# Moving a fold from GpSimd to VectorE in spread pieces, and halving the block sums, in a mixer kernel

## The chip, the cores and the metric

The kernel runs on one core of a Trainium2 chip; every trace and result lists that core alone. The metric is the device time of one execution in microseconds (us), lowest is best. Every kernel is timed beside runs of the kernel before on the same chip. Engines: PE is TensorE's matrix multiply, PEld its weight load, DVE is VectorE, ACT is ScalarE, POOL is GpSimd, SP is the engine that only issues DMAs here.

## The reference, cut to what matters

```python
X = np.fft.fft(x, axis=1); X = np.fft.fft(X, axis=2); x = X.real   # x: 8 x 3008 x 256
xt = x.transpose(0, 2, 1)
h = np.maximum(xt @ w_tok1, 0.0) @ w_tok2        # token mixing, 3008 -> 256 -> 3008
u = x + h.transpose(0, 2, 1)
h2 = np.maximum(u @ w_ch1, 0.0) @ w_ch2          # channel mixing, 256 -> 1536 -> 256
return (u + h2).astype(np.float32)
```

The kernel works batch by batch. While TensorE does the channel mixing of batch b (six chunks of 512 tokens, the last of 448, each in four "places" s = 0 to 3, so 24 places a batch), the Fourier front end of batch b+1 is woven in, and before that the input x of batch b+2 is *folded*: x[t] plus or minus x[-t], which halves the work of the transform.

## The kernel before

Three parts matter. The first is the fold, 12 pieces a batch, on whatever engine is handed in. Every operand is fp16 in SBUF:

```python
def fold(b, engs):
    ...
    for s, (t0, t1) in enumerate(((13, 17), (9, 13), (5, 9), (1, 5))):
        tt = engs[s].tensor_tensor
        ...
        tt(out=xp[:, t, 1:D], in0=xp[:, t, 1:D], in1=xm[0:KR, rv, D - 1:0:-1], op=add)   # L423
        yield
        ...
        tt(out=eo[:, t, 1:129], in0=xp[:, t, 1:129], in1=xp[:, t, 255:127:-1], op=add)   # L429
        yield
        tt(out=eo[:, t, 129:256], in0=xp[:, t, 1:128], in1=xp[:, t, 255:128:-1], op=sub) # L431
        yield
```

The second is the block sums on VectorE. The second channel product is done with seven block products instead of eight, which needs four sums of blocks of the hidden layer c1 in each of 42 of the 48 chunks (the other six, `plain` in the code, take the eight products). All operands are in SBUF again:

```python
def hidden_sums(c1, sb, k, which):
    ...
    sums = ((sb[:, 0, k], a21, a22, AT.add),                 # sb<-c
            (sb[:, 1, k], sb[:, 0, k], a11, AT.subtract),    # sb<-sb,c
            (a21, a11, a21, AT.subtract),                    # c<-c
            (sb[:, 2, k], a12, sb[:, 1, k], AT.subtract))    # sb<-c,sb
    for i in which:
        o, x, y, op = sums[i]
        nc.vector.tensor_tensor(out=o, in0=x, in1=y, op=op)  # L609
```

The third is the second product. TensorE's results are added up by VectorE out of PSUM (`residual(v, ...)`), and GpSimd adds the transposed u, `rt`, from SBUF to SBUF (`residual(g, ...)`, both L618). VectorE first copies some edge columns of `rt` (`edges`, L613). PSUM for this product has only two buffers, so TensorE waits when VectorE's residual add is late (13 waits, 23.5 us in all, in the trace of this kernel).

```python
elif s == 2:
    product(pa[:, 0], lambda k: c1[:, k], 1, lambda k: wst[:, 2, k])
    keep(2)
    residual(v, osb[:, 2:4, upper], pb[:, 0], m[:, 2])
else:
    product(pa[:, 0], ...); product(pb[:, 0], ...)
    residual(v, osb[:, 2:4, lower], pa[:, 0], rt[:, 2:4, lower])
    residual(v, osb[:, 0:2, upper], pb[:, 0], m[:, 1])
    residual(g, osb[:, :, upper], osb[:, :, upper], rt[:, :, turned_])
```

The main loop before: fold 1 runs on GpSimd ahead of the loop, folds 2 to 7 two pieces a place from place 10 (batch 0: 15), and the four block sums of a chunk run whole in places 0 and 1 of the next chunk.

## Time and profile before

643.45 us, median of 3 runs (643.16 to 644.06).

| | before |
|---|---|
| PE busy | 595.9 us, 93% of the span (642.3 us, the profiled run) |
| DVE, ACT, POOL busy | 482.5, 442.7, 296.9 us |
| batches 0 to 7 | 74.5, 77.4, 77.8, 76.9, 77.7, 74.9, 71.2, 67.2 us |
| PE gaps in them | 3.0, 4.5, 5.7, 5.7, 4.5, 3.8, 0, 0.1 us |

A batch is measured from its first up-projection matmul (L592) to that of the next; batch 7 ends with PE's last work. A gap is the time from the end of PE's last matmul to the start of its next; the ends are modelled.

From the page of the kernel before: the engines' busy time, and the busy tenths in 40 equal slices. PEclk is the granted clock in tenths.

```profile
PE 595.9 (93%) x6322; PEld 425.1 (66%) x6322; DVE 482.5 (75%) x820; ACT 442.7 (69%) x996; POOL 296.9 (46%) x261
...
PE   2899989998899988999888998999989999999997
POOL 8459269337932378104991159601692211111121
PEclk9999989999899999999999999899999999999999
```

PE is the bound. After start-up it falls to 8 in nine slices, and in eight of these POOL is at 6 or more; but in three of the seven slices in which POOL reaches 9, PE stays at 9. In three places the clock falls too, to 0.5 for 3.41 us each.

Windows cut at the batches (kernel before; start:end, length, then busy us and instruction count of each engine, granted clock, DMA share, GB/s): batches 1, 2, 6 and 7.

```profile
core 0: us, PE busy (x) PEld busy (x) DVE busy (x) ACT busy (x) POOL busy (x), PEclk, DMA share, GB/s
114.40:191.80 77.40, 72.95 (x757) 51.21 (x756) 57.14 (x93) 51.91 (x119) 41.04 (x34) 0.98 0.57 102
191.80:269.60 77.80, 72.09 (x806) 51.81 (x805) 63.85 (x96) 52.92 (x122) 39.20 (x32) 1.00 0.39 83
499.00:570.30 71.30, 71.30 (x806) 51.68 (x805) 52.89 (x96) 52.76 (x122) 12.28 (x12) 1.00 0.33 68
570.30:637.50 67.20, 67.14 (x673) 47.69 (x671) 44.19 (x76) 42.99 (x88) 13.60 (x11) 1.00 0.35 76
```

Batches 2 and 6 do the same work on PE (806 matmuls), yet batch 2 takes 6.5 us more. DVE runs the same 96 instructions in both, and is busy 63.85 us in one and 52.89 in the other. The difference between the batches is the fold on POOL, with the load of x that batch 2 issues behind it; batch 5 folds and issues no load, and still has 3.8 us of gaps.

The list of PE's waits (kernel before; total us, times, longest):

```profile
PE px L633 <- DVE osb L618: 23.5, 13, 2.9
PE pt L265 <- ACT tp L249: 11.7, 1, 11.7
```

The second line is start-up. The first is nearly the whole of what the batches lose.

Groups of instructions by form (kernel before; out<-in, count, busy us, mean ns, then idle time before them):

```profile
L609 DVE TENSOR_TENSOR sb<-sb,c 128x1536 f16<-128x1536 f16 x42 | 64.7, 1540 | 1.4
L609 DVE TENSOR_TENSOR c<-c 128x1536 f16<-128x1536 f16 x42 | 50.8, 1211 | 0.0
L613 DVE COPY rt<-rt 128x4 f16<-128x4 f16 x72 | 28.8, 400 | 0.8
...
L423 POOL TENSOR_TENSOR xp<-xp,xm 94x1020 f16<-94x1020 f16 x28 | 66.3, 2367 | 7.2 <-PE filler L283 7.2
```

The means hide two populations. A sum that no POOL op overlaps takes 0.95 us; one that POOL ops cover for 95% or more takes 1.5 to 2.1 us on average, by kind of sum. VectorE's adds out of PSUM take the same alone and so covered: 0.42 us for 128x256 (`osb`), 0.69 for 128x512 (`ut`).

One such case in the timeline of the kernel before (start us, length us; lines picked from it):

```profile
164.73 1.86 POOL L431 TENSOR_TENSOR eo<-xp 94x508 f16<-94x508 f16 x1
165.78 2.92 DVE L613 COPY rt<-rt 128x4 f16<-128x4 f16 x2
166.18 0.83 PE L633 MATMUL py<-wst,sb 128*128 128x128 f16 x12
166.56 2.11 POOL L423 TENSOR_TENSOR xp<-xp,xm 94x1020 f16<-94x1020 f16 x1
168.61 0.41 DVE L618 TENSOR_TENSOR osb<-px,m 128x256 f32<-128x256 f32 x1
169.07 0.44 PE L633 MATMUL px<-wst,sb 128*128 128x128 f16 x5 [2.06 <-DVE osb L618]
```

Two copies of four columns, 0.17 us each when undisturbed, last until the fold piece is done. The residual add behind them is 2 us late, and PE stands for 2.06 us.

### The profile page before, as it was taken

Reading aid. Unit: us, or ns where it says so; the run is one execution under the profiler, and the core shown is the slowest. Engines: PE = TensorE matmul, PEld = TensorE weight load, DVE = VectorE, ACT = ScalarE, POOL = GpSimd, SP = SyncE. Lnnn points to the kernel's source line nnn. Section 1 sums busy time; section 2 is a strip of 40 time slices with the busy share of each in tenths; the row PEclk is TensorE's granted clock in tenths of the full one; section 3 lists DMA queues with packets and bytes.
Section 4 is the critical chain, followed back from the end, with each engine's and each line's share of the span. In section 5 each row is a group of like instructions: output and inputs, shape, how many; then the busy total and the mean of one; then the engine's idle time right before and its main releaser. Section 6 shows DMA issues by size and latency. Waiting matters only on the chain.

```text
span 642.3 us, 15533 instructions
## 1 busy us (share of the span) xinstructions
PE 595.9 (93%) x6322; PEld 425.1 (66%) x6322; DVE 482.5 (75%) x820; ACT 442.7 (69%) x996; POOL 296.9 (46%) x261
## 2 busy tenths in 40 slices
PE   2899989998899988999888998999989999999997
PEld 1766667665677656766666665776667767766675
DVE  8667678569777798757979589765997766776764
ACT  8766966676568765777665866668667777766672
POOL 8459269337932378104991159601692211111121
PEclk9999989999899999999999999899999999999999
DMA  9993921952353325352264322832403342322423
GB/s 141 210 181 87 174 50 35 166 83 59 59 126 82 85 51 103 90 99 50 51 119 112 70 57 44 172 72 49 94 17 73 66 92 59 72 62 58 96 55 97
DMA packets 86599, 56.51 MB, mean 88 GB/s; under 512 B 54864, under 2 KB 83472, under 8 KB 85776
## 3 DMA queue, kind: packets, MB, share of 16 engines
q1 hardware_dynamic: 78048, 37.84, 28.5%
q0 software_dynamic: 8256, 17.49, 15.7%
q8 instruction: 49, 0.80, 0.5%
q10 hardware_dynamic: 224, 0.20, 0.1%
q14 instruction: 22, 0.18, 0.1%
HBM read 34.98 MB, written 24.64 MB: 93 GB/s over the span
## 4 chain that ended last, share of the span: by engine, by line
PE 74%; DVE 13%; issue 5%; ACT 5%; POOL 2%; DVEq 0%; POOLq 0%
PE pc L592 31%; PE px L633 18%; PE py L633 6%; PE pu L552 6%; PE po L690 4%; DVE sb L609 3%; PE pt L488 3%; DVE c L609 2%; DVE osb L618 2%; PE pz L445 2%; ACT c L595 1%; DVE ut L560 1%; DVE rt L613 1%; DVE ut L544 1%; POOL xp L423 1%
## 5 line engine op out<-in xcount | busy, mean ns | idle before, releaser
L595 ACT ACTIVATE c<-pc 128x512 f16<-128x512 f32 (+1 forms) x572 | 296.4, 595 | 41.7 <-PE pc L592 22.1
L618 POOL TENSOR_TENSOR osb<-osb,rt 128x256 f32<-128x256 f32 x84 | 89.6, 1067 | 312.7 <-DVE osb L618 303.2
L592 PE MATMUL pc<-ut,wc1p 128*128 128x512 f16 x576 | 140.3, 379 | 0.0
L592 PE MATMUL pc<-ut,wc1m 128*128 128x512 f16 (+1 forms) x576 | 137.9, 376 | 0.0
L633 PEld LDWEIGHTS <-c 128*128 128x128 f16 x2016 | 121.2, 98 | 23.8 <-DVE c L609 5.7
L633 PEld LDWEIGHTS <-sb 128*128 128x128 f16 x1512 | 91.1, 98 | 34.5 <-issue 22.9
L638 ACT ACTIVATE m<-px 128x256 f32<-128x256 f32 x126 | 48.5, 385 | 94.5 <-PE px L633 71.0
L560 DVE TENSOR_TENSOR ut<-pu,yt 128x512 f16<-128x512 f32 (+1 forms) x96 | 64.3, 672 | 31.5 <-PE pu L552 31.3
L592 PEld LDWEIGHTS <-wc1m 128*128 128x128 f16 x576 | 53.7, 99 | 47.9 <-issue 3.0
L592 PEld LDWEIGHTS <-wc1p 128*128 128x128 f16 x576 | 52.2, 98 | 49.0 <-issue 2.2
L633 PE MATMUL px<-wst,c 128*128 128x128 f16 x1008 | 70.5, 220 | 2.5 <-DVE c L609 2.1
L423 POOL TENSOR_TENSOR xp<-xp,xm 94x1020 f16<-94x1020 f16 x28 | 66.3, 2367 | 7.2 <-PE filler L283 7.2
L609 DVE TENSOR_TENSOR sb<-sb,c 128x1536 f16<-128x1536 f16 x42 | 64.7, 1540 | 1.4
L633 PE MATMUL px<-wc,c 128*128 128x128 f16 x1008 | 63.1, 219 | 0.0
L609 DVE TENSOR_TENSOR sb<-c 128x1536 f16<-128x1536 f16 x42 | 54.4, 1295 | 7.5 <-ACT c L595 7.5
L633 PE MATMUL px<-wst,sb 128*128 128x128 f16 x504 | 36.0, 222 | 23.5 <-DVE osb L618 23.5
L609 DVE TENSOR_TENSOR sb<-c,sb 128x1536 f16<-128x1536 f16 x42 | 53.6, 1277 | 0.0
L290 ACT ACTIVATE z<-pz 128x480 f16<-128x480 f32 (+1 forms) x60 | 40.1, 674 | 18.9 <-PE pz L445 9.8
L618 DVE TENSOR_TENSOR osb<-py,m 128x256 f32<-128x256 f32 x84 | 35.4, 422 | 23.5 <-ACT m L638 13.0
L609 DVE TENSOR_TENSOR c<-c 128x1536 f16<-128x1536 f16 x42 | 50.8, 1211 | 0.0
L552 PE MATMUL pu<-w2p,uu 128*128 128x512 f16 (+1 forms) x168 | 50.3, 379 | 0.2 <-ACT uu L510 0.2
L431 POOL TENSOR_TENSOR eo<-xp 94x508 f16<-94x508 f16 (+1 forms) x28 | 44.2, 1578 | 0.0
(168 smaller groups left out, 762.9 us busy)
## 6 DMA issues: line engine op xcount, KB each, us to landing
out_dram<-osb SPq DMA_DIRECT2D x83, 256.0 KB, 3.5
xp<-in_x_dram POOLq DMA_DIRECT2D x16, 272.0 KB
out_dram<-osb SPq DMA_DIRECT2D x11, 192.0 KB, 3.2
xp<-in_x_dram POOLq DMA_DIRECT2D x16, 127.5 KB
rt<-ut SPq DMA_TRANSPOSE x96, 3.1
w2s<-in_moe_w_tok_dram POOLq DMA_DIRECT2D x1, 1504.0 KB
w1p<-in_moe_w_tok_dram POOLq DMA_DIRECT2D x2, 384.0 KB
wc<-in_moe_w_ch_dram POOLq DMA_DIRECT2D x1, 768.0 KB
```

Source lines behind the costliest of these rows:

```text
L290: nc.scalar.activation(out=out_, in_=in_, func=AFT.Copy)
L423: tt(out=xp[:, t, 1:D], in0=xp[:, t, 1:D], in1=xm[0:KR, rv, D - 1:0:-1], op=add)
L431: tt(out=eo[:, t, 129:256], in0=xp[:, t, 1:128], in1=xp[:, t, 255:128:-1], op=sub)
L552: nc.tensor.matmul(pu[:, 0:n], lhsT=uu[:, th, int(minus), h, :], rhs=w2_cols(b, c)[:, th], start=(th == 0), stop=(th == 1))
L560: nc.vector.tensor_tensor(out=ut[:, h, 0:n].rearrange("p (a b) -> p a b", b=64), in0=pu[:, 0:n].rearrange("p (b a) -> p a b", b=64), in1=y ...
L592: nc.tensor.matmul(pc[:, 0:n], lhsT=wc[:, h, ct * P:(ct + 1) * P], rhs=ut[:, h, 0:n], start=(h == 0), stop=(h == 1))
L595: nc.scalar.activation(out=c1[:, ct, 0:n], in_=pc[:, 0:n], func=AFT.Relu)
L609: nc.vector.tensor_tensor(out=o, in0=x, in1=y, op=op)
L618: eng.tensor_tensor(out=o, in0=x, in1=y, op=AT.add)
L633: nc.tensor.matmul(o[:, t], lhsT=a(k)[:, f:f + P], rhs=w(k), start=(first and t == 0 and k == 0), stop=(k == HC - 1), skip_group_check=True)
L638: nc.scalar.activation(out=m[:, i], in_=pa[:, 0], func=AFT.Copy)
L690: nc.tensor.matmul(po[0:n, o:o + D], lhsT=c1[:, ct, ks * P:ks * P + n], rhs=wc2[:, ct, :], start=(ct == 0), stop=(ct == NCT - 1))
```

## The change

Its intent: take the fold off GpSimd, where it disturbs VectorE, and give it to VectorE in pieces so small and so spread that VectorE can take them; and split the block sums so that half of them run while the chunk's own relus still come, rather than all in the first half of the next chunk. The core of the diff:

```diff
-    if BB > 1:
-        take(fold(1, [nc.gpsimd] * 4), 12)
-    if BB > 2:
-        x_tiles[2] = load_x(2)
+    early = fold(1, [nc.vector] * 4)
...
-        folds = fold(b + 2, [nc.gpsimd] * 4) if b + 2 < BB else None
+        folds = fold(b + 2, [nc.vector] * 4) if b + 2 < BB else None
...
-                sums = prev is not None and not plain(*prev[0:2])
-                if s == 0 and sums:
-                    hidden_sums(prev[2], pbox["sb"], slice(0, HC), (0, 1))
+                if s < 2 and prev is not None and not plain(*prev[0:2]):
+                    block_sums(prev[2], pbox["sb"], slice(3, HC), (2 * s, 2 * s + 1))
...
-                if s == 1 and sums:
-                    hidden_sums(prev[2], pbox["sb"], slice(0, HC), (2, 3))
                 if prev is not None:
                     mm2(*prev, s, pbox)
+                if s >= 2 and not plain(b, c):
+                    block_sums(c1, box["sb"], slice(0, 3), (2 * s - 4, 2 * s - 3))
...
-                if b == 0 and sub == 5:
+                if b == 0 and sub == 4:
                     weight_sums()
...
+                if b == 0 and 3 <= sub < 9:
+                    take(early, 2)
+                    if sub == 8:
+                        x_tiles[2] = load_x(2)
                 if folds is not None and sub >= fold_at[b > 0]:
-                    take(folds, 2)
-                    if sub == fold_at[b > 0] + 5 and b + 3 < BB:
+                    take(folds, 1 + (b == 0))
+                    if sub == fold_at[b > 0] + (5 if b == 0 else 11) and b + 3 < BB:
                         x_tiles[b + 3] = load_x(b + 3)
```

(`block_sums` is `hidden_sums` renamed.) So the change has three parts: the *engine* of the fold, its *spread* (one piece a place over twelve places instead of two over six, from batch 1 on), and the *halves*. Some small moves come with them: fold 1 goes from ahead of the loop into places 3 to 8 of batch 0, the loads of x and the weight sums change places.

More of the change, by code (lines that the diff above doesn't have):

```diff
@@ L597, in mm1, with block_sums @@
                 ts(c1[:, ct, 0:n], pc[:, 0:n], 0.0, AT.max)
-    def hidden_sums(c1, sb, k, which):
+    def block_sums(c1, sb, k, which):
         hi = slice(HC + k.start, HC + k.stop)
```

## The prediction

The sum is 610 us as the ceiling (643.45 us less about 33) and 6 to 7 us given back, 616.

> **What bounds it now.** TensorE. On the page PE is busy 595.9 us of 642.3 (93%) and holds 74% of the chain of waits. By windows cut at each batch's first up-projection matmul (L592), the batches take 74.5, 77.4, 77.8, 76.9, 77.7, 74.9, 71.2 and 67.2 us. Batches 6 and 7 run no fold, and PE has no gap there. In batches 0 to 5 its gaps sum to 3.0, 4.5, 5.7, 5.7, 4.5 and 3.8 us, 27 us in all, nearly all in the second half of a batch, where GpSimd folds. The list of waits puts 23.5 us of PE's down to VectorE's residual add (`px <- osb`, L618). After three gaps the granted clock is 0.6-0.8 for about 4 us (near 90, 171, 404 us), some 5 us more.
>
> **Why VectorE is late.** A block sum takes 0.95 us with GpSimd idle; covered by a GpSimd op 1.5-2.1 us, longest 2.9. A 4-column edge copy goes from 0.17 to 1.2 us. Ops with an operand in PSUM (0.42, 0.69 us) don't change. [...] At 165.8 us two edge copies take 2.9 us beside a fold, the residual add follows, PE waits 2.06 us.
>
> **What the change moves.**
> - Folds of batches 1 to 7 leave GpSimd: about 164 of its 297 us. The residual adds (about 12 us a batch) and loads of x stay.
> - VectorE gets them. Its fold of batch 0 shows the price: 0.68, 0.43, 0.41 us a piece (2.4, 1.6, 1.6 on GpSimd), 6.8 us a batch, 47 us in all.
> - Each block sum becomes two. The weight sums (128x768, 0.56 us undisturbed) give the price: 2 x 0.56 against 0.95, at most 27 us over 168 sums, about half as back-to-back ops overlap by 0.08 us.
> - VectorE loses the fold's stretch: 63.8 us busy in batch 2, 52.9 in batch 6, so about 10 us a batch.
> VectorE's total stays near 480-510 us. TensorE's work is unchanged.
>
> **Critical path.** Against about 71.1 us (batch 6; batch 5 less its gap), batches 1 to 5 lose 6.3, 6.7, 5.8, 6.6 and 3.8 us, 29 us; batch 0 loses 3 to 4. Ceiling about 33 us, so 610. I give back about 1 us a batch, since VectorE nears 90% in chunks 2 to 5 and GpSimd's residual adds still stretch some sums, and 1 to 2 us in batch 0, where the early fold, the weight sums and the new halves fall into 16 us of a VectorE already full.
>
> **Predicted: 616 us, range 608 to 627 (8 in 10).** Faster by over 2%: 0.93; within 2%: 0.06; slower: 0.01.
>
> **Right if** batches 1 to 5 take 71 to 73 us; PE's waits on `osb` fall from 23.5 to under 6 us; GpSimd is busy 130-140 us; a half sum takes about 0.56 us, a few stretched beside L618 on GpSimd; no clock drop after 100 us; batches 6 and 7 stay within 1 us. What is left lies at 45 to 65 us and in chunks 3 to 5.
>
> **Wrong if** VectorE is full in chunks 2 to 5, so that sums or `ut` come late (then 625-635); if GpSimd's residual adds stretch the many smaller ops more than the larger; if fold 1 ends late and batch 1's front or batch 2's load waits; or if an unbroken TensorE draws a lower clock, which batches 6 and 7 (139 us near 1.0) don't show.

## The result, and the profile after

617.39 us, median of 4 runs (616.26 to 618.29), against 643.75 us (643.16 to 645.24, 4 runs). The ratio is 0.9586, 95% interval 0.9561 to 0.9612: 4.1% faster. Ratios here are the mean time of one kernel's runs over that of the other's runs of the same rounds, so not quite the ratio of the medians quoted.

From the page of the kernel after, the same lines as before:

```profile
PE 589.1 (96%) x6322; PEld 422.5 (69%) x6322; DVE 492.8 (80%) x1086; ACT 442.0 (72%) x996; POOL 139.3 (23%) x163
...
PE   2899999999999999999999999999999999999996
POOL 8500413111142121302114221311121212101121
PEclk9999999999999999999999999999999999999999
```

POOL lost 157.6 us of work, DVE gained 10.3 us in all, and no slice of PE or of its clock falls below 9 between start-up and the last slice. That the time falls by 26 us while PE's busy time falls by only 7 is no contradiction: most of the gain is PE's idle time (its gaps in batches 0 to 5 fall from 27.1 to 5.5 us). Of the 7 us of busy time the clock is about 5, by an estimate: the trace of the kernel before has three stretches of 3.41 us in the batches in which the granted clock is 0.5, that of the kernel after has none.

Windows of batches 1, 2, 6 and 7 (kernel after):

```profile
110.30:181.60 71.30, 70.97 (x758) 50.60 (x757) 57.63 (x127) 51.75 (x119) 13.65 (x15) 1.00 0.42 80
181.60:254.40 72.80, 71.74 (x805) 51.79 (x804) 62.94 (x134) 52.88 (x122) 17.26 (x19) 1.00 0.44 89
470.10:542.00 71.90, 71.51 (x805) 51.75 (x804) 57.45 (x120) 52.88 (x122) 12.97 (x12) 1.00 0.33 67
542.00:609.30 67.30, 67.11 (x672) 47.65 (x671) 47.42 (x96) 43.01 (x88) 12.54 (x11) 1.00 0.39 76
```

The eight batches take 71.9, 71.2, 72.9, 71.6, 72.9, 71.2, 71.9 and 67.3 us. DVE does the whole fold in batch 2 (134 instructions instead of 96) and is busy *less* than before, 62.94 against 63.85 us. PE's waits (kernel after):

```profile
PE px L633 <- DVE osb L618: 2.6, 8, 0.8
PE pz L445 <- DVE ut L560: 1.6, 3, 0.7
```

From the groups by form (kernel after):

```profile
L609 DVE TENSOR_TENSOR sb<-c,sb 128x768 f16<-128x768 f16 x84 | 84.4, 1004 | 0.0
L609 DVE TENSOR_TENSOR c<-c 128x768 f16<-128x768 f16 x84 | 49.5, 590 | 0.0
L609 DVE TENSOR_TENSOR sb<-sb,c 128x768 f16<-128x768 f16 x84 | 46.9, 558 | 2.9
L609 DVE TENSOR_TENSOR sb<-c 128x768 f16<-128x768 f16 x84 | 45.9, 547 | 2.4 <-ACT c L595 2.4
L613 DVE COPY rt<-rt 128x4 f16<-128x4 f16 x72 | 13.3, 184 | 0.8
```

The edge copies are free of the stretch (184 ns against 400). The half sums are at 0.55 to 0.59 us, but for one kind, `sb<-c,sb`, whose mean is 1.00 us. The timeline of the kernel after, at the start of batch 2, shows what holds it (lines picked from it):

```profile
182.01 0.41 DVE L618 TENSOR_TENSOR osb<-py,m 128x256 f32<-128x256 f32 x1
182.34 0.56 DVE L609 TENSOR_TENSOR c<-c 128x768 f16<-128x768 f16 x1
182.83 2.05 DVE L609 TENSOR_TENSOR sb<-c,sb 128x768 f16<-128x768 f16 x1
183.27 1.17 POOL L618 TENSOR_TENSOR osb<-osb,rt 128x512 f32<-128x512 f32 x1
184.79 0.68 DVE L560 TENSOR_TENSOR ut<-pu,yt 128x512 f16<-128x512 f32 x1
185.53 0.37 PE L445 MATMUL pz<-t1n,eo 94*128 94x96 f16 x5 [0.72 <-DVE ut L560]
```

GpSimd's own residual add is released by VectorE's residual add, so it starts just when the half sums behind that add run. The add of `ut` comes late, and PE waits 0.72 us for it. Chunk 0 of batches 2 and 4 takes 13.29 us in place of 12.04; g1 below takes this cause away, and chunk 0 is back at 12.04.

### The profile page after: what moved, and what is told of

Read it like the earlier page. It is cut to its first block, busy times and chain, and to the rows that moved or that the text cites. A ratio compares the mean times of both kernels' runs of the same rounds, so it can differ in the third digit from the quotient of the medians.

```text
span 614.2 us, 15694 instructions
## 1 busy us (share of the span) xinstructions
PE 589.1 (96%) x6322; PEld 422.5 (69%) x6322; DVE 492.8 (80%) x1086; ACT 442.0 (72%) x996; POOL 139.3 (23%) x163
## 4 chain that ended last, share of the span: by engine, by line
PE 80%; DVE 8%; ACT 6%; issue 3%; POOL 1%; DMA 1%; DVEq 0%; POOLq 0%
PE pc L592 33%; PE px L633 20%; PE py L633 7%; PE pu L552 6%; PE po L690 4%; PE pt L488 3%; ACT c L595 3%; DVE sb L609 2%; DVE osb L618 2%; PE pz L445 1%; PE pw L472 1%; PE pw L473 1%; DVE ut L560 1%; PE py L519 1%; DVE yt L526 1%
## 5 line engine op out<-in xcount | busy, mean ns | idle before, releaser
L618 POOL TENSOR_TENSOR osb<-osb,rt 128x256 f32<-128x256 f32 x84 | 92.2, 1097 | 438.5 <-DVE osb L618 411.4
L592 PE MATMUL pc<-ut,wc1m 128*128 128x512 f16 (+1 forms) x576 | 134.9, 370 | 0.0
L609 DVE TENSOR_TENSOR sb<-c,sb 128x768 f16<-128x768 f16 x84 | 84.4, 1004 | 0.0
L618 DVE TENSOR_TENSOR osb<-py,m 128x256 f32<-128x256 f32 x84 | 35.4, 422 | 29.4 <-ACT m L638 23.2
L609 DVE TENSOR_TENSOR c<-c 128x768 f16<-128x768 f16 x84 | 49.5, 590 | 0.0
L609 DVE TENSOR_TENSOR sb<-sb,c 128x768 f16<-128x768 f16 x84 | 46.9, 558 | 2.9
L609 DVE TENSOR_TENSOR sb<-c 128x768 f16<-128x768 f16 x84 | 45.9, 547 | 2.4 <-ACT c L595 2.4
L475 DVE SCALAR_TENSOR_TENSOR w<-alt,pw 128x131 f16<-128x131 f16 x96 | 33.0, 350 | 14.4 <-ACT w L290 14.3
L526 DVE TENSOR_TENSOR yt<-py,qs 128x512 f16<-128x512 f32 x48 | 30.8, 683 | 8.8 <-ACT qs L522 8.8
```

Of the source, the lines that this page charges most:

```text
L475: nc.vector.scalar_tensor_tensor(out=w[:, g, 0:131], in0=alt[:], scalar=pw[:, 131:132], in1=pw[:, 0:131], op0=AT.mult, op1=AT.add)
L526: nc.vector.tensor_tensor(out=yt[:, h, CW * c:CW * c + CW], in0=py[:], in1=qs[:], op=op)
L592: nc.tensor.matmul(pc[:, 0:n], lhsT=wc[:, h, ct * P:(ct + 1) * P], rhs=ut[:, h, 0:n], start=(h == 0), stop=(h == 1))
L618: eng.tensor_tensor(out=o, in0=x, in1=y, op=AT.add)
```

## The experiments

Theory A: while GpSimd reads SBUF, VectorE's ops with two SBUF inputs and its edge copies are stretched (in before the sums go from 0.95 to 1.5-2.1 us beside its ops, the copies from 0.17 to 1.2); the residual adds then come late and PE waits. That it is the read of SBUF is a supposition at this point, which e5 and e6 test. Rivals: B, the gain comes from the halves and the even spread, whatever engine folds; C, GpSimd's queue was too long, so its residual adds and stores came late.

### The engine, the spread and the halves one by one

The three parts can each be on or off, which makes eight kernels. Six were built beside before and after. All but e3 were made from the kernel after and so keep its small moves (fold 1 inside the loop, the loads, the weight sums); a comparison of e7 or e8 with before has these in it, one among e1, e2, e4, e7, e8 and after does not, but for the loads of x, which go with the spread.

e1_engine, one word undone in two places:

```diff
-    early = fold(1, [nc.vector] * 4)
+    early = fold(1, [nc.gpsimd] * 4)
-        folds = fold(b + 2, [nc.vector] * 4) if b + 2 < BB else None
+        folds = fold(b + 2, [nc.gpsimd] * 4) if b + 2 < BB else None
```

> The changed kernel with one word undone: all folds of batches 1 to 7 go back to GpSimd; the halves, the spread places and the new load places stay. Theory A (GpSimd's folds stretch VectorE's two-input ops and edge copies): most of the gain goes, 636 to 648 us; block halves beside a fold well over 0.56 us; PE gaps of 3 us or more in each of batches 1 to 5. Rival B (the halves and the even spread made the gain, whatever engine folds): 615 to 622 us.

e2_fold_only, the block sums whole again:

```diff
-                    block_sums(prev[2], pbox["sb"], slice(3, HC), (2 * s, 2 * s + 1))
+                    block_sums(prev[2], pbox["sb"], slice(0, HC), (2 * s, 2 * s + 1))
-                if s >= 2 and not plain(b, c):
-                    block_sums(c1, box["sb"], slice(0, 3), (2 * s - 4, 2 * s - 3))
```

> The changed kernel with the block sums whole again, in their old places; folds on VectorE, spread. Theory A: keeps nearly all of the gain, 614 to 622 us. Rival B: loses half or more of it, 628 us or more. If the halves cost VectorE more than they return, this run is at or below the changed kernel's 617.

e3_halves_only is the kernel before with only the two `block_sums` hunks of the change and the place of the weight sums.

> The kernel before with only the block sums halved (and the weight sums one place earlier, as the change has them); folds stay on GpSimd, two pieces a place. Theory A: within 1% of before, 637 to 648 us. Rival B: 630 us or less.

e4_burst, the spread undone:

```diff
-                    take(folds, 1 + (b == 0))
-                    if sub == fold_at[b > 0] + (5 if b == 0 else 11) and b + 3 < BB:
+                    take(folds, 2)
+                    if sub == fold_at[b > 0] + 5 and b + 3 < BB:
```

> The changed kernel with the folds of VectorE not spread: two pieces a place for six places, as before, load of x six places earlier. If the spread matters (VectorE is near full in chunks 2 to 4 and a pair of pieces delays the residual adds): 619 to 624 us, with new PE gaps in chunk 3 or 4. If it doesn't: within 1.5 us of the changed kernel.

e7_spread_only is e2 with both folds on `nc.gpsimd`; e8_engine_only is e2 with the edit of e4.

> Folds on GpSimd, but in the changed kernel's spread places (one piece a place over twelve); block sums whole as before. With e1 (0.9855 of before, with halves) it tells the part of the spread. Theory A (each piece beside VectorE costs a stretch, and two in one place cost PE a wait that one doesn't): 632 to 640 us, near e1. If the halves made e1's gain: 642 to 648.

> Folds on VectorE in the old bursts of two pieces a place, block sums whole. With e4 (halves, 0.975 of before) it tells whether halves hurt in a burst. Theory A: the engine alone gives about half of the gain, 622 to 632 us, with PE gaps left in chunks 3 and 4; the halves cost VectorE about 1.3 us a batch there, so this is some us under e4.

Measured (each ratio is to the kernel before on the same chip, whose median was 643.75 us beside after, 645.54 beside e1 to e4 and 644.02 beside e5 to e8; 95% interval in brackets; batches 1 to 5, and the sum of PE's gaps in each of them, from the traces):

| kernel | fold on | pieces | sums | median us | ratio | batches 1-5, us | PE gaps in each, us |
|---|---|---|---|---|---|---|---|
| before | GpSimd | burst | whole | 643.75 | 1 | 74.9-77.8 | 3.8-5.7 |
| e3 | GpSimd | burst | halves | 665.05 | 1.0305 (1.0279-1.0331) | 79.7-82.2 | 7.1-7.4 |
| e7 | GpSimd | spread | whole | 633.77 | 0.9843 (0.9826-0.9859) | 74.1-75.4 | 3.0-3.4 |
| e1 | GpSimd | spread | halves | 635.96 | 0.9855 (0.9827-0.9884) | 74.0-75.9 | 2.7-3.6 |
| e8 | VectorE | burst | whole | 626.32 | 0.9733 (0.9708-0.9759) | 72.5-73.3 (one 79.0) | 1.3-1.5 (one 5.2) |
| e4 | VectorE | burst | halves | 628.93 | 0.9750 (0.9706-0.9794) | 73.6-75.1 | 2.4-2.9 |
| e2 | VectorE | spread | whole | 618.41 | 0.9585 (0.9568-0.9602) | 71.8-72.4 | 0.7-0.8 |
| after | VectorE | spread | halves | 617.39 | 0.9586 (0.9561-0.9612) | 71.2-72.9 | 0.3-1.1 |

What follows:

- The engine gives 2.6 to 2.7% with whole sums (e8 against before; e2 against e7) and the spread 1.5 to 1.6% (e7 against before; e2 against e8). With whole sums they add up; neither alone is the change. (The spread alone is under 2%, but its interval excludes 1.) Theory A as stated put the gain down to the engine alone, and e1 came out at the edge of what it allowed (635.96 us, expected 636 to 648; gaps of 3 us or more expected, 2.7 to 2.8 found in batches 1, 3 and 5): a part of the gain is the spread, on whichever engine. In e7's trace PE's wait on `px <- osb` is 11.1 us instead of 23.5, and of the three stretches of low clock one is left. e2, e7 and e8 lie in their expected ranges; e4 missed its range of 619 to 624 us on the slow side.
- The halves give nothing: e2 and after have the same ratio, and so, within their intervals, have e1 and e7, and e4 and e8. In the one place where they matter they hurt: with GpSimd folding in bursts (e3) they cost 3%. That is against both expectations, 637 to 648 and under 630. In e3 the four kinds of sums take 110.1 + 64.6 + 62.5 + 54.2 = 291 us of VectorE, before 223.5. The 336 halves need 185 us undisturbed (measured in h2 below) and the 168 whole sums about 160, so the stretch grew from 64 to 106 us. The clock takes its part too: in e3's batches it is at 0.5 for 27.3 us, in before for 10.2, an estimate of 8.5 us of the loss. By an estimate from these numbers the stretch is 0.38 us a whole sum before and 0.32 us a half in e3: nearly as much an op, and there are twice as many ops. Why the shorter op does not lose less was not shown.
- Busy time does not tell the cost. e4 and after have equal VectorE time (492.3 and 492.8 us) and differ by 1.7%. In e4 the list of waits has 8.4 us of PE on `px <- osb` and 5.3 us on `py <- sb`; after has 2.6 us and none. (Its profiled run also has two stretches of 3.41 us at clock 0.5; two of its four runs, at 627.3 and 627.4 us, show a granted clock of 1.0 and are still slower than after.) The timeline of e4_burst shows a sum and then PE waiting behind the pair of pieces of one place (with fold pieces L429 and L431 in front of the sum):

```profile
160.71 0.49 DVE L429 TENSOR_TENSOR eo<-xp 94x640 f16<-94x640 f16 x1
161.11 0.48 DVE L431 TENSOR_TENSOR eo<-xp 94x635 f16<-94x635 f16 x1
161.51 0.55 DVE L609 TENSOR_TENSOR sb<-c 128x768 f16<-128x768 f16 x1
162.12 0.68 PE L633 MATMUL py<-wst,sb 128*128 128x128 f16 x9 [1.06 <-DVE sb L609]
```

- The one long batch of e8 is a stop of PE of 3.9 us inside a group of matmuls for which the profile names no releaser; after it the granted clock is 0.5 for 6.83 us. It is in the profiled run (628.97 us); the three others took 625.5 to 626.8.

### Is it the read of SBUF, or the length of GpSimd's queue?

Both kernels are the changed kernel with useless work on GpSimd in the places of VectorE's fold pieces, on a tile of zeros of its own.

```diff
+    da = work.tile([KR, 4, 255], FP16, tag="da", name="da")
+    nc.vector.memset(da[:], 0.0)
     ...
                     take(early, 2)
+                    beside(2)
     ...
                     take(folds, 1 + (b == 0))
+                    beside((1 + (b == 0)) * (sub < fold_at[b > 0] + (6 if b == 0 else 12)))
```

In e5_read each `beside` is `nc.gpsimd.tensor_tensor(da += da)`, 94x1020 or 94x508 as the fold piece was. In e6_write it is one or two `nc.gpsimd.memset(da, 0.0)` of 94x1020. The fills take three quarters of the adds' time (106.2 us, 948 ns each, against 139.9), so GpSimd's queue is not quite as long as in e5.

> The changed kernel, and beside each fold piece of VectorE a useless add on GpSimd, of the fold's old size, that reads SBUF (a tile of zeros that nothing else uses). Theory A (a stretch by two engines that both read SBUF): the gain goes again, 636 to 655 us; the sums and the fold pieces beside it stretched to 1 us and more, the PSUM ops not. Rival C (GpSimd's queue was too long, so its residual adds and stores came late): as long too.

> As e5, but GpSimd fills the tile with zeros in place of adding: about the same time on GpSimd (some 1 us for each fill of 1020 elements), no read of SBUF. Theory A: VectorE's sums are not stretched beyond the changed kernel's, 616 to 622 us; the edge copies may be. Rival C (GpSimd's queue is what costs): as slow as e5, 636 us or more.

| kernel | median us | ratio | the useless work on GpSimd |
|---|---|---|---|
| e5_read | 667.22 | 1.0359 (1.0333-1.0384) | 84 adds, 139.9 us |
| e6_write | 619.21 | 0.9612 (0.9593-0.9632) | 112 fills, 106.2 us |

Groups by form of e5_read:

```profile
L609 DVE TENSOR_TENSOR sb<-c 128x768 f16<-128x768 f16 x84 | 63.2, 752 | 2.3 <-ACT c L595 2.3
L774 POOL TENSOR_TENSOR da<-da 94x508 f16<-94x508 f16 x56 | 76.1, 1359 | 2.5
L774 POOL TENSOR_TENSOR da<-da 94x1020 f16<-94x1020 f16 x28 | 63.8, 2278 | 8.3 <-PE pc L592 7.5
```

The same groups of e6_write:

```profile
L609 DVE TENSOR_TENSOR sb<-c 128x768 f16<-128x768 f16 x84 | 45.9, 546 | 2.3 <-ACT c L595 2.3
L774 POOL MEMSET da<- 94x1020 f16 x112 | 106.2, 948 | 10.6 <-DVE da L766 6.5
```

Over 100 us of fills on GpSimd leave VectorE's sums where they were in the changed kernel (546 against 547 ns; all four kinds together 226.7 us in both) and the intervals of the times overlap. The adds make the mean 752 ns (all kinds 272.5 us) and cost more than the whole change had won; VectorE's ops with an operand in PSUM stay at 0.42 and 0.67 us, as expected. Theory A stands and rival C falls: in these runs VectorE's sums keep their time beside 106.2 us of GpSimd work that only writes SBUF, and lose it beside 139.9 us that reads SBUF too. e5 is slower than before, and slower than I expected (636 to 655 us), probably since here VectorE carries the fold as well as the stretch: it is busy 561.3 us, against 482.5 before. No run separates the two.

The edge copies are another matter. Only two of e6's 72 meet a fill, and both, 0.44 and 0.60 us long, end within 0.04 us of its end. The second, behind a sum that the same fills leave alone (timeline of e6_write, lines picked from it):

```profile
98.18 2.95 POOL L774 MEMSET da<- 94x1020 f16 x3
99.62 0.56 DVE L609 TENSOR_TENSOR sb<-sb,c 128x768 f16<-128x768 f16 x1
100.56 0.81 DVE L613 COPY rt<-rt 128x4 f16<-128x4 f16 x2
```

So for these copies a GpSimd op that only writes is enough; two cases are few, and they cost nothing that the times show.

### Versions that go further

g1_sums_first moves the first-half sums ahead of the residual adds:

```diff
+                if s >= 2 and not plain(b, c):
+                    block_sums(c1, box["sb"], slice(0, 3), (2 * s - 4, 2 * s - 3))
                 if prev is not None:
                     mm2(*prev, s, pbox)
-                if s >= 2 and not plain(b, c):
-                    block_sums(c1, box["sb"], slice(0, 3), (2 * s - 4, 2 * s - 3))
```

> The changed kernel, with the first-half block sums of places 2 and 3 ahead of the second product's residual adds on VectorE instead of behind them. In the changed kernel the residual add of GpSimd starts right after VectorE's residual add and catches the half sum behind it (mean 1.00 us against 0.55); batches 2, 4 and 6 lose about 1.2 us in chunk 0 to it. If that is so: chunk 0 of the even batches back to about 12.0 us, that sum's mean under 0.75 us, 612 to 615 us (ratio to before 0.951 to 0.955). If the order matters to nothing: 616 to 618. If the residual adds come late behind the sums: over 619.

g2_earlier is g1 with `fold_at = [15, 8]` in place of `[15, 10]`; h1_whole_earlier is e2 with the same edit.

> g1, and the folds of batches 1 and later two places earlier (places 8 to 19 of 24), which frees chunk 5, where VectorE has the most work. If chunk 5 is short of VectorE: 0.2 to 0.8 us a batch less than g1 in batches 1 to 5, 1 to 4 us in all (ratio 0.947 to 0.954). Otherwise as g1.

> e2 (folds on VectorE and spread, whole block sums) with the folds two places earlier. In e2 chunk 5 takes 12.7 us in odd and 12.6 in even batches against 11.85 in batch 6. If the two fold pieces there are the cause: chunk 5 back to about 11.9, 613 to 616 us (ratio 0.951 to 0.956), as good as the changed kernel with no half sums at all.

h2_no_gpsimd is g1 with `v, g = nc.vector, nc.vector`, so that GpSimd computes nothing in the loop.

> g1, with the residual adds of rt on VectorE too, so that GpSimd only issues loads. Takes away the rest of the contention: every half sum near 0.55 us, which in g1 average 0.59 to 0.69 (336 sums, 216 us; undisturbed about 185), so 30 us less; but 84 fp32 adds come to VectorE, an estimate of 0.3 to 0.7 us each from the 0.28 and 0.42 us of its adds of 128 and 256 elements out of PSUM, 42 us. About even for VectorE's total: 612 to 620 us. If the contention that is left still cost PE waits, faster than g1 (under 612); if VectorE is the tight engine, slower (over 618).

| kernel | median us | ratio | batches 1-5, us |
|---|---|---|---|
| (before, beside g1, g2, h1: 643.93; beside h2: 644.14) | | 1 | |
| g1_sums_first | 613.63 | 0.9535 (0.9513-0.9557) | 71.5-71.7 |
| g2_earlier | 615.55 | 0.9565 (0.9542-0.9588) | 71.8-72.2 |
| h1_whole_earlier | 615.93 | 0.9557 (0.9534-0.9580) | 71.4-71.8 |
| h2_no_gpsimd | 612.75 | 0.9495 (0.9446-0.9543) | 71.3-71.4 |

g1 did what was expected: chunk 0 of the even batches is back at 12.04 us, and the mean of `sb<-c,sb` is 633 ns instead of 1004. The contention did not all go, it partly moved: the sums at the start of the next chunk now meet the add (`sb<-c` 661 ns, `sb<-sb,c` 689). All sums together fell from 226.7 to 216.1 us.

g2 missed (ratio 0.9565, expected 0.947 to 0.954): chunk 5 of the odd batches did not get shorter but took up to 13.0 us (g1: 12.6 to 12.75), so two fold pieces there are not its cause. h1 is within its range, but by half only: chunk 5 is down to 12.0 us in the even batches, and 12.2 to 12.6 in the odd. What holds the odd ones was not found; in g1 and h2 0.60 us of their extra 0.76 or so is a wait of PE for VectorE's residual add (`py <- osb`), in h1 there is no such wait.

h2 is the cleanest view of theory A. Groups by form, h2_no_gpsimd:

```profile
L609 DVE TENSOR_TENSOR sb<-c,sb 128x768 f16<-128x768 f16 x84 | 46.2, 550 | 0.0
L618 DVE TENSOR_TENSOR osb<-osb,rt 128x512 f32<-128x512 f32 x42 | 29.1, 693 | 1.4
L618 DVE TENSOR_TENSOR osb<-osb,rt 128x256 f32<-128x256 f32 x42 | 17.8, 425 | 1.4
```

Every half sum is at 0.55 us (185.4 us in all). VectorE took 46.9 us of adds that had cost GpSimd 86.2 us in g1, and its own total is 485.2 us, against 486.2 in g1 and 492.8 in the changed kernel: handing the work to GpSimd had saved VectorE nothing. h2 is about 1% faster than the changed kernel by the ratios to before (they ran in different jobs, and the intervals do not overlap). It is not told apart from g1. h2 and g1 beat both kernels, the changed one by less than 2%.

## Why the prediction was right

It said 616 us, 608 to 627; the median is 617.39. Point by point:

- *The bound and the ceiling.* The estimate rested on batches 6 and 7, the ones without a fold: 71.1 us for batches 1 to 5, and about 1 us given back in each. They take 71.2 to 72.9. PE's wait on `osb` was to fall from 23.5 us to under 6 and is 2.6.
- *The cause.* Stretch of VectorE's sums by GpSimd's reads: shown by e1 (the folds back on GpSimd), by e6 against e5 (546 against 752 ns for `sb<-c`), and by h2 (all half sums at 0.55 us).
- *The busy times.* GpSimd 130 to 140 us (139.3), VectorE 480 to 510 us (492.8). The prices were those of ops that GpSimd leaves alone: in h2 the folds of batches 1 to 7 take VectorE 46.6 us (predicted 47) and a half sum 0.55, but in the changed kernel GpSimd's residual adds stretch both, to 56.6 us and a mean of 0.67.
- *The clock.* No drop after 100 us: right. (The 0.6-0.8 that the prediction quotes for before are means over some 4 us; the trace has 0.5 for 3.41 us, three times.) Batches 6 and 7 within 1 us: 71.9 and 67.3 against 71.2 and 67.2.
- *A miss: "a few stretched beside L618 on GpSimd".* 46 of 84 sums of the kind `sb<-c,sb` take more than 0.6 us, and the mean of the kind is 1.00. This costs chunk 0 of batches 2 and 4 1.25 us each, a place that the prediction did not name. It named 45 to 65 us instead, and there the chunks of batch 0 take what they took before (7.65, 11.99, 11.78 us). So the "about 1 us a batch" given back (0.1 to 1.8 in batches 1 to 5, mean 0.9) was right in size and mostly wrong in place, and that part is luck. One of the "wrong if" came true as well, without harm: the adds stretch the sums by 41 us in the changed kernel, by 25 in e2 with whole ones, at the same ratio.
- *A gap in the argument.* The prediction counted the move to VectorE as the whole gain, with the spread as a mere condition. e8 and e7 show that the engine alone is worth 2.7% and the spread 1.6%. The total came out right because it was read from a ceiling, not from the parts; had the pieces not been spread as well, e4 and e8 say 626 to 629 us, at the end of the range or beyond it. The halves were counted as a cost only; e2 says that they neither cost nor give here.

## What to carry to other kernels

Before giving work to an idle GpSimd, ask whether it reads SBUF while VectorE runs ops with two SBUF inputs (and, for copies like these, whether it writes it). Here a half sum (`sb<-c`) took 547 ns, 546 beside added fills on GpSimd and 752 beside added adds, and 86 us of adds on GpSimd came back to VectorE as 47 us of work and the total did not rise, because as much stretch went. Look in the trace for a stretch in which the suspected cost is absent (here the last two batches) and take the ceiling from it; then ask not only how much work an engine gets but what stands in front of what in its queue, since e4 and the changed kernel differ by 1.7% with the same busy time. A change of several parts should be taken apart: of these three, one gave nothing.

## What the traces show of the clock and of single ops

- In before the granted clock is 0.5 for 3.41 us from 91.46, 169.97 and 402.07 us: the starts are 23.0 and 68.0 times 3.413 us apart. In the 3.41 us just ahead of them PE was idle for 2.28, 2.06 and 2.26 us. Lay a grid of 3.413 us through these starts: a gap of 2.59 us at 247 us falls across two of its windows, at most 1.69 us in one, and the clock stays at 1.00. Over the batches of the traces of before and after, each on a grid through its own low clock (after has one, past its last matmul), the three windows at full clock with 2.06 us or more of idle PE were followed by the low clock, and none of the 335 with 1.84 us or less was. So here 2 us of idle PE went with a low clock where they fell into one window (ends of matmuls are modelled, so the limit is rough); the cause was not shown.
- The fold piece starts one fp16 element into its row and takes VectorE 0.68 us for 1020 elements. A line through the undisturbed sums of 768 and 1536 elements (0.55 us in h2, 0.95 us in before) gives an estimate of 0.68 us: the odd start costs nothing that these times show.
- Beside a GpSimd add a half sum of 0.55 us took up to 2.05 us (after, at 182.83 us).
- On GpSimd the fold piece of 1020 elements took 2.11 us at its fastest and 2.37 us in the mean (before, 28 pieces).
